# An attention and gMLP block on one core: loads placed behind the end of a unit's turns, and two pairs of neighbouring units by rows in each group

## Chip, cores, metric

The kernel runs on one core of one Trainium2 chip. The metric is the device time of one execution in microseconds (us), as the median of several executions.

## The reference, cut to what matters

```python
x = A_x                                       # 2048 x 512, bf16
# ... (sa, ca, ga, sb, cb, gb) = six vectors of 512 from silu(c) @ w_mod
h = _layernorm(x) * (1 + ca) + sa
q = (h @ wq)                                  # 32 heads of 128; 8 groups of 4 heads share one K, V
scores = einsum('bhqd,bhkd->bhqk', q, k) * Dh ** (-0.5)      # 2048 keys
o = einsum('bhqk,bhkd->bhqd', softmax(scores), v)
x = x + ga * (o @ wo)                         # o: 2048 x 4096
# ... then layernorm and a gMLP: gelu, layernorm over half the channels,
#     a 2048 x 2048 product over positions, a gate, an output product
```

The attention is some 85% of the time, and the change is in it alone.

## The kernel before: the parts that matter

The attention is cut into 128 **units**: 8 groups (one K, V head each) of 16 units, a unit being 128 queries for the four heads of a group. One pass of the main loop, an **iteration**, has eight slots. In a slot TensorE computes an eighth of the scores of the newest unit, an eighth of a V product of an earlier unit, and one matmul of the query or output projection. ScalarE takes the exponential of the slot's scores. Groups and the units of a group are numbered from 0; groups 1 to 6 are the steady middle.

There are two kinds of units. A unit **by columns** gets its scores transposed (keys on partitions), so that its V product can follow at once; but this product needs 64 matmuls of 129 columns. A unit **by rows** gets scores with queries on partitions; each head's rows are normalised on VectorE and then transposed by DMA (a **turn**, four of them per unit). After that its V product needs only 16 matmuls of 512 columns.

```python
TURN_A, TURN_B = 2 * CT, NU - 2                 # 8 and 126
def by_rows(u):
    return TURN_A <= u < TURN_B and u % 2 == 0
def pv_at(u):                                   # iteration of the V product
    return u + 3 if by_rows(u) else u + 1
def wo_at(u):                                   # iteration of the output projection
    return pv_at(u) + (3 if u < TURN_B - CT else 2)
# ...
# in qk(u, i), by rows: two score matmuls, one exponential with its row sum
    nc.scalar.activation(out=rows_of(u, hh)[...], in_=s_ps[:], func=ACT.Exp,
        scale=inv_sqrt_dh, accum_out=rsums[u][:, i : i + 1])
    if half == 1:                               # a head is complete: its turn, two slots later
        at(*divmod(u * NSLOT + i + 2, NSLOT), lambda: turn_rows(u, hh))
# ...
def turn_rows(u, hh):
    # ... tot, reciprocal, rows * rinv on VectorE
    nc.sync.dma_start_transpose(out=pTs[u][:, :, hh * P : (hh + 1) * P], in_=rows)
# ...
# in pv(u, i), by columns, at the last slot: the unit's output is turned as well
    nc.sync.dma_start_transpose(out=oTs[u][:], in_=onorms[u][:].rearrange("p r d -> p (r d)"))
# ...
for g in range(1, HKV):                         # loads of the next groups, on GpSimd's and SyncE's queues
    it = (g - 1) * NT
    at(it + 9, 5, lambda g=g: load_k(g))
    at(*((5, 2) if g == 1 else (it + 7, 4)), lambda g=g: load_wq(g, nc.gpsimd))
    at(*((5, 2) if g == 1 else (it + 11, 4)), lambda g=g: load_v(g))
    at(*((5, 2) if g == 1 else (it + 13, 4)), lambda g=g: load_wo(g, nc.gpsimd))
```

`at(it, slot, fn)` puts a piece of program at a slot. The score banks `s_ps` are two. In the profile lines, the buffers `pT` and `wsp` hold what a V product reads, and `pn`, `win_sb` and `wmod_a` rows that are not turned yet; `x2` marks two instructions merged into one line.

## Time and profile before

| | |
|---|---|
| time | 1314.3 us median of 4 (1313.1 to 1316.1) |
| TensorE busy | 99% |
| ScalarE, VectorE busy | 85%, 53% |
| groups 1 to 6 (iterations 16 to 111) | 837.1 us, 139.52 each |
| DMA engines, mean share in groups 2 to 6 | 0.79 |

The length of a group is the sum of its iterations, and an iteration runs from its first score weight load to the next one's. The view of stretches for groups 2 to 6 of the kernel before: its columns are the stretch and its length, then busy us (and instructions) of TensorE, its weight loads, VectorE, ScalarE and GpSimd, then the granted TensorE clock, the DMA share and GB/s.

```profile
288.38:985.98 697.60, 692.55 (x5026) 395.47 (x5121) 339.47 (x840) 680.60 (x961) 13.65 (x19) 1.00 0.79 143
```

697.60 us for five groups is 139.52 each.

### The profile page before, as it was taken

How to read it: one execution, taken by the hardware profiler on the slowest of the kernel's cores; microseconds unless marked ns; L12 is line 12 of the kernel's file. 1: busy time of each engine (PE TensorE's matmuls, PEld its weight loads, DVE VectorE, ACT ScalarE, POOL GpSimd, SP SyncE). 2: the span in 40 equal slices, each digit the busy share in tenths (PEclk: the TensorE clock that was granted, in tenths of full speed). 3: DMA queues.
4: the chain of work that ended last, by engine and by line, in shares of the span. 5: the costliest groups of instructions: out<-in, count | busy, mean ns of one | idle time of the engine just before them, and what ended most of it. 6: DMA issues, size and time to landing. Idle time of an engine off the chain costs nothing.

```text
span 1312.3 us, 24168 instructions
## 1 busy us (share of the span) xinstructions
PE 1294.0 (99%) x9355; PEld 736.5 (56%) x9527; DVE 689.3 (53%) x1693; ACT 1113.0 (85%) x1533; POOL 55.7 (4%) x96
## 2 busy tenths in 40 slices
PE   9999999999999999999999999999999999999998
PEld 5665555555555555555555555555555555644445
DVE  5644545444445554444545444444454588784444
ACT  7899999999999999999999999999999999550000
POOL 1200000000000000000000000000000011120000
PEclk9999999999999999999999999999999999999999
DMA  6599778878787787879886788678866688365300
GB/s 181 122 117 179 127 142 144 156 122 149 153 161 140 139 142 141 142 138 140 157 162 121 143 142 156 125 146 153 153 130 127 117 143 149 96 134 96 82 21 27
DMA packets 607723, 174.45 MB, mean 133 GB/s; under 512 B 597264, under 2 KB 603664, under 8 KB 607600
## 3 DMA queue, kind: packets, MB, share of 16 engines
q1 hardware_dynamic: 600576, 153.67, 66.1%
q0 software_dynamic: 4432, 16.91, 4.9%
q10 hardware_dynamic: 2592, 2.23, 0.5%
q8 instruction: 77, 1.26, 0.4%
q14 instruction: 46, 0.38, 0.1%
HBM read 21.89 MB, written 2.10 MB: 18 GB/s over the span
## 4 chain that ended last, share of the span: by engine, by line
PE 96%; DMA 1%; issue 1%; DVE 1%; ACT 0%; SPq 0%; POOL 0%; DVEq 0%; ACTq 0%
PE o_ps L1080 19%; PE s_ps L1024 18%; PE s_ps L1005 16%; PE o_ps L1059 15%; PE misc L1112 8%; PE misc L945 8%; PE misc L1437 7%; PE s_ps L1271 2%; PE s_ps L1310 2%; PE o_ps L1458 1%; DMA wsp<-in_w_mod_dram 1%; PE s_ps L1458 0%; DMA kT<-in_A_k_cache_dram 0%; DVE hT L814 0%; DMA hT<-xn 0%
## 5 line engine op out<-in xcount | busy, mean ns | idle before, releaser
L1031 ACT ACTIVATE pT<-s_ps 128x1024 bf16<-128x1024 f32 x552 | 561.1, 1025 | 31.5 <-PE s_ps L1024 9.5
L1080 PEld LDWEIGHTS <-pT 128*128 128x128 bf16 x4416 | 295.3, 98 | 128.9
L1080 PE MATMUL o_ps<-v,pT 128*128 128x129 bf16 x4416 | 339.7, 220 | 1.5
L1024 PE MATMUL s_ps<-qT,kT 128*128 128x512 bf16 x1104 | 328.1, 379 | 1.4 <-ACT pT L1031 0.2
L1005 PE MATMUL s_ps<-kT,qT 128*128 128x512 bf16 x917 | 274.9, 379 | 3.0
L1012 ACT ACTIVATE win_sb<-s_ps 128x1024 bf16<-128x1024 f32 x238 | 243.7, 1025 | 3.5
L1112 PE MATMUL misc<-wo_g,oT 128*128 128x512 bf16 x468 | 177.4, 379 | 0.6
L945 PE MATMUL misc<-hT,wq_g 128*128 128x512 bf16 (+2 forms) x482 | 173.3, 370 | 0.8
L1024 PEld LDWEIGHTS <-kT 128*128 128x128 bf16 x1104 | 107.2, 98 | 115.0 <-issue 2.3
L1012 ACT ACTIVATE pn<-s_ps 128x1024 bf16<-128x1024 f32 x156 | 159.6, 1025 | 2.0 <-ACT wmod_a L1012 0.3
L1059 PEld LDWEIGHTS <-v 128*128 128x128 bf16 x944 | 92.3, 98 | 111.5
L956 DVE CAST qT<-misc 128x512 bf16<-128x512 f32 x125 | 85.7, 685 | 122.9 <-PE misc L945 122.8
L1068 DVE CAST oT<-o_ps 128x512 bf16<-128x512 f32 x59 | 40.8, 692 | 194.9 <-PE o_ps L1059 157.4
L1059 PE MATMUL o_ps<-wsp,v 128*128 128x512 bf16 x457 | 137.1, 379 | 0.6
L1059 PE MATMUL o_ps<-pT,v 128*128 128x512 bf16 x441 | 133.0, 379 | 0.6
L1005 PEld LDWEIGHTS <-qT 128*128 128x128 bf16 x944 | 92.2, 98 | 61.6
L1045 DVE TENSOR_TENSOR tot<-rs 128x1 f32<-128x1 f32 x236 | 36.2, 153 | 127.2 <-ACT win_sb L1012 84.8
L1437 PE MATMUL misc<-wsp,z 128*128 128x512 bf16 (+2 forms) x554 | 101.1, 336 | 0.6 <-issue 0.2
L1050 DVE TENSOR_SCALAR win_sb<-win_sb,rall 128x2048 bf16<-128x2048 bf16 x119 | 89.6, 753 | 4.4 <-DVE rall L1048 0.3
L1012 ACT ACTIVATE wmod_a<-s_ps 128x1024 bf16<-128x1024 f32 x78 | 79.9, 1024 | 0.0
L1437 PEld LDWEIGHTS <-z 128*128 128x128 bf16 x560 | 50.5, 98 | 49.3 <-DVE z L686 1.4
L1125 DVE TENSOR_TENSOR xacc<-misc,xacc 128x512 f32<-128x512 f32 x112 | 76.1, 680 | 0.0
(107 smaller groups left out, 817.3 us busy)
## 6 DMA issues: line engine op xcount, KB each, us to landing
wq_g<-in_A_wq_dram POOLq DMA_DIRECT2D x7, 512.0 KB, 6.2
v<-in_A_v_cache_dram POOLq DMA_DIRECT2D x7, 512.0 KB, 6.9
wo_g<-in_A_wo_dram POOLq DMA_DIRECT2D x7, 512.0 KB, 8.4
wsp<-in_w_mod_dram POOLq DMA_DIRECT2D x1, 2048.0 KB, 11.2
out_dram<-yout ACTq DMA_DIRECT2D x16, 128.0 KB, 1.7
win_sb<-in_B_w_in_dram POOLq DMA_DIRECT2D x1, 1792.0 KB, 8.0
x_sb<-in_A_x_dram SPq DMA_DIRECT2D x3, 512.0 KB, 5.9
oT<-onorm SPq DMA_TRANSPOSE x69, 2.8
```

What stands on the lines that cost most here:

```text
L945: nc.tensor.matmul(ps[0][:, o0 : o0 + n], lhsT=wqs[g][:, dt, hh * DH : (hh + 1) * DH], rhs=hTs[ch][:, dt, c0 : c0 + n], start=(dt == 0), s ...
L956: nc.vector.tensor_copy(out=dst, in_=src)
L1005: nc.tensor.matmul(s_ps[:, c * 512 : (c + 1) * 512], lhsT=qTs[b][:, hh, jj * P : (jj + 1) * P], rhs=groups[g]["kT"][:, k0 : k0 + 512], sta ...
L1012: nc.scalar.activation(out=rows_of(u, hh)[:, half * HK : (half + 1) * HK], in_=s_ps[:], func=ACT.Exp, scale=inv_sqrt_dh, accum_out=rsums[u ...
L1024: nc.tensor.matmul(s_ps[:, h * 512 : (h + 1) * 512].rearrange("p (r q) -> p r q", r=REP), lhsT=groups[g]["kT"][:, kt * P : (kt + 1) * P], ...
L1031: nc.scalar.activation(out=pTs[u][:, 2 * i : 2 * i + 2, :], in_=s_ps[:].rearrange("p (k q) -> p k q", k=2), func=ACT.Exp, scale=inv_sqrt_dh,)
L1050: nc.vector.tensor_scalar(out=rows, in0=rows, scalar1=rinv, scalar2=None, op0=ALU.mult)
L1059: nc.tensor.matmul(o_pss[u][:], lhsT=groups[g]["v1"][:, kt, 0:DH], rhs=pTs[u][:, kt, :], start=(kt == 0), stop=(kt == NKT - 1),)
L1080: nc.tensor.matmul(o_ps[:, hh % 2, 0 : DH + 1], lhsT=pTs[u][:, kt, hh * P : (hh + 1) * P], rhs=groups[g]["v1"][:, kt, 0 : DH + 1], start=( ...
L1112: nc.tensor.matmul(X_ps[:], lhsT=oTs[u][:, hh, :], rhs=groups[g]["wo"][:, hh, :], start=(hh == 0), stop=(hh == REP - 1),)
L1125: nc.vector.tensor_tensor(out=xaccs[j][:], in0=X_ps[:], in1=xaccs[j][:], op=ALU.add)
L1437: nc.tensor.matmul(g_ps[:, :n], lhsT=z2[:, st, f * P : (f + 1) * P], rhs=wsp[t][:, st, c0 : c0 + n], start=(st == 0), stop=(st == NT - 1 a ...
```

## The change

Its intent: more units by rows (59 become 65, by making units 4, 5 and 13, 14 of groups 1 to 6 neighbours by rows), which saves TensorE time (an iteration with a V product by rows took 8.63 us, one by columns 8.81); some V products after two iterations, to keep one per iteration; the load of K two iterations later; and the loads of V, wq and wo held back until the last turn of a certain unit has landed, by a copy on GpSimd that reads what that turn writes.

```diff
-    def by_rows(u):
-        return TURN_A <= u < TURN_B and u % 2 == 0
-    def pv_at(u):
-        return u + 3 if by_rows(u) else u + 1
+    kinds, pv_its = [False] * NU, {}
+    for u in range(TURN_A, TURN_B):
+        pair = NT <= u < NU - NT and u % NT in (5, 6, 13, 14) and not kinds[u - 2]
+        kinds[u] = not kinds[u - 1] or pair
+    by_rows, order = kinds.__getitem__, [(u + 3 if kinds[u] else u + 1, u) for u in range(NU)]
+    order.sort()
+    for it in range(1, NU + 2):
+        due = [u for t, u in order if t <= it]
+        if not due and it > TURN_A + 1:
+            due = [u for t, u in order if t <= it + 1 and kinds[u]]
+        for u in due[: 2 if it > TURN_B else 1]:
+            pv_its[u] = it
+            order = [o for o in order if o[1] != u]
+    pv_at = pv_its.__getitem__
 ...
+    def after_rows(u):
+        seen = stat.tile([1, 1], BF16, name="seen")
+        nc.gpsimd.tensor_copy(out=seen[:], in_=pTs[u][0:1, NKT - 1, 511:512])
+    def after_pv(u):
+        seen = stat.tile([1, 1], FP32, name="seen")
+        nc.gpsimd.tensor_copy(out=seen[:], in_=rall[0:1, u * REP : u * REP + 1])
+    at(5, 0, lambda: after_pv(3))
     for g in range(1, HKV):
         it = (g - 1) * NT
-        at(it + 9, 5, lambda g=g: load_k(g))
-        at(*((5, 2) if g == 1 else (it + 7, 4)), lambda g=g: load_wq(g, nc.gpsimd))
-        at(*((5, 2) if g == 1 else (it + 11, 4)), lambda g=g: load_v(g))
-        at(*((5, 2) if g == 1 else (it + 13, 4)), lambda g=g: load_wo(g, nc.gpsimd))
+        at(it + 11, 5, lambda g=g: load_k(g))
+        loads = (load_v(g), load_wq(g, nc.gpsimd), load_wo(g, nc.gpsimd))   # (as lambdas)
+        for k, load in enumerate(loads):
+            if g == 1:
+                at(5, 0, load)
+                continue
+            u = next(u for u in range(it + 4 + 2 * k, NU) if by_rows(u))
+            at(u + 1, 5, lambda u=u: after_rows(u))
+            at(u + 1, 5, load)
```

(The bookkeeping of row buffers and of which units are looked at in an iteration is left out.)

More of the change, by code (lines that the diff above doesn't have):

```diff
@@ L966 @@
     TURN_A, TURN_B = 2 * CT, NU - 2
-    def by_rows(u):
-        return TURN_A <= u < TURN_B and u % 2 == 0
-    def pv_at(u):
-        return u + 3 if by_rows(u) else u + 1
+    kinds, pv_its = [False] * NU, {}
[11 more added lines that the diff above has]
+            order = [o for o in order if o[1] != u]
+    assert len(pv_its) == NU
+    pv_at = pv_its.__getitem__
     def wo_at(u):
@@ L979 @@
     for u in range(NU):
-        homes[u] = min(users, key=lambda k: users[k])
+        homes[u] = min(users, key=users.get)
         assert users[homes[u]] < u
@@ L1038, in rows_of @@
     def rows_of(u, hh):
-        return pn[((u - TURN_A) // 2 * REP + hh) % len(pn)][:, 0:SK]
+        return pn[(sum(kinds[:u]) * REP + hh) % len(pn)][:, 0:SK]
     def turn_rows(u, hh):
@@ L1254 @@
         at(NU + 1 + st // 4, 2 * (st % 4), lambda st=st: load_wsp(wsp[0], 0, st))
+    def after_rows(u):
[5 more added lines that the diff above has]
+    at(5, 0, lambda: after_pv(3))
     for g in range(1, HKV):
         it = (g - 1) * NT
-        at(it + 9, 5, lambda g=g: load_k(g))
-        at(*((5, 2) if g == 1 else (it + 7, 4)), lambda g=g: load_wq(g, nc.gpsimd))
-        at(*((5, 2) if g == 1 else (it + 11, 4)), lambda g=g: load_v(g))
-        at(*((5, 2) if g == 1 else (it + 13, 4)), lambda g=g: load_wo(g, nc.gpsimd))
+        at(it + 11, 5, lambda g=g: load_k(g))
+        loads = (
+            lambda g=g: load_v(g),
+            lambda g=g: load_wq(g, nc.gpsimd),
+            lambda g=g: load_wo(g, nc.gpsimd),
+        )
+        for k, load in enumerate(loads):
[5 more added lines that the diff above has]
+            at(u + 1, 5, load)
     zs = {}
@@ L1361 @@
             zs["z2"] = z2p.tile([P, NT, FH], BF16, name="z2")
-        pvs = [u for u in (it - 5, it - 3, it - 1) if 0 <= u < NU and pv_at(u) == it]
-        wos = [u for u in range(max(it - 6, 0), min(it - 2, NU)) if wo_at(u) == it]
+        pvs = [u for u in range(max(it - 4, 0), min(it, NU)) if pv_at(u) == it]
+        wos = [u for u in range(max(it - 8, 0), min(it - 2, NU)) if wo_at(u) == it]
         wf = [fn for u in wos for fn in wo_proj(u)]
```

## The prediction

> **What bounds the kernel now.** I read the page first, then the timeline of the middle, then the waits and the landings of DMAs.
>
> The page of the kernel before, engine shares (part 1) and the chain that ended last (part 4):
>
> ```profile
> PE 1294.0 (99%) x9355; PEld 736.5 (56%) x9527; DVE 689.3 (53%) x1693; ACT 1113.0 (85%) x1533; POOL 55.7 (4%) x96
> ...
> PE 96%; DMA 1%; issue 1%; DVE 1%; ACT 0%; SPq 0%; POOL 0%; DVEq 0%; ACTq 0%
> ```
>
> TensorE is 99% busy and 96% of the chain, but a modelled end can hide gaps, so I look at starts. In the timeline of TensorE and ScalarE in the fifth of eight groups (start us, length us, what), one unit by rows (L1005, 602.51 to 611.32) is followed by one by columns (L1024, 611.32 to 619.95):
>
> ```profile
> 602.51 0.59 PE L1005 MATMUL s_ps<-kT,qT 128*128 128x512 bf16 x2
> 602.94 0.62 PE L1080 MATMUL o_ps<-v,pT 128*128 128x129 bf16 x8
> 603.40 0.38 PE L945 MATMUL misc<-hT,wq_g 128*128 128x512 bf16 x1
> 603.61 0.59 PE L1005 MATMUL s_ps<-kT,qT 128*128 128x512 bf16 x2
> ...
> 611.32 0.59 PE L1024 MATMUL s_ps<-qT,kT 128*128 128x512 bf16 x2
> 611.75 0.59 PE L1059 MATMUL o_ps<-pT,v 128*128 128x512 bf16 x2
> 612.18 0.38 PE L945 MATMUL misc<-hT,wq_g 128*128 128x512 bf16 x1
> 612.40 0.59 PE L1024 MATMUL s_ps<-qT,kT 128*128 128x512 bf16 x2
> ...
> 619.95 0.59 PE L1005 MATMUL s_ps<-kT,qT 128*128 128x512 bf16 x2
> ```
>
> Each turn of the loop ("iteration", eight slots) computes one unit's scores (L1005 by rows, L1024 by columns) and the product with V of an earlier unit. The V product of a unit by columns is eight 129-column matmuls a slot (603.40 - 602.94 = 0.46 us, 57 ns each). That of a unit by rows is two of 512 columns (612.18 - 611.75 = 0.43 us). So a slot lasts 1.10 or 1.08 us and an iteration 8.81 or 8.63 us, with every start butting on the one before. I worked out all 128 iterations this way, from the weight loads of L1005 and L1024, of which none is missing: in groups 1 to 6 (numbered from 0) they are 8.81 and 8.63 without one exception, 139.52 us a group. **In these groups TensorE waits for nothing.** That includes the moments when loads collide with turns (a turn is the transpose of one head's rows by DMA):
>
> ```profile
> 611.79 0.76 POOL L739 DMA_DIRECT2D wo_g<-in_A_wo_dram  x1 [24.66 <-PE misc L1112]
> ```
> ```profile
> 616.12 7.26 SPq L1051 DMA_TRANSPOSE wsp<-wmod_a  x1
> 624.05 4.90 SPq L1051 DMA_TRANSPOSE pT<-pn  x2
> ```
>
> The load of wo starts as soon as the old buffer is free, the fourth turn of unit 68 is then issued for 7.26 us (1.3 to 3.5 is usual) and lands 24.6 us after that unit's scores began. Its V product comes three iterations after, at 26.1 us, so nothing is lost. Of the landings of a fourth turn I list: unit 4 of a group (wo collides) 18.5 to 24.6 us, unit 10 (wq collides) 17.6 to 22.2; units 6, 12 and 14, with no load near, 18 cases, median 17.5, mean 17.7, longest 18.3.
>
> [...] one 512 KB load from the POOL queue put off a turn by up to 7 us. [...] Here 57 and 216 are what a sustained stream shows[...].
>
> **The change part by part.**
> (1) *More units by rows.* Running the schedule's few lines by hand gives 59 units by rows before and 65 after: one more in each of the six groups 1 to 6. Neighbours by rows are units 4, 5 and 13, 14 of each. Each extra one replaces 64 matmuls of 129 columns by 16 of 512 (the built program has 576 fewer rows on TensorE: 6 x 48 matmuls with their weight loads, twice). On the path it is worth 8.81 - 8.63 = 0.18 us: **6 x 0.18 = -1.1 us**. It adds four multiplies of 0.75 us on VectorE (53% busy) and four turns of some 2.4 us of DMA, both beside the matmuls; the DMA engines' mean share in the groups goes from about 0.80 to an estimate of 0.86.
> (2) *Two iterations per group (12 in all) have scores by rows and a V product by rows.* There ScalarE may be the slower:
>
> ```profile
> 603.14 1.02 ACT L1012 ACTIVATE win_sb<-s_ps 128x1024 bf16<-128x1024 f32 x1
> 604.06 0.20 ACT L1012 ACTIVATION_READ_ACCUMULATOR win_sb<-s_ps 128x1 f32 x1
> 604.24 1.02 ACT L1012 ACTIVATE win_sb<-s_ps 128x1024 bf16<-128x1024 f32 x1
> ```
>
> An exponential with its row sum takes 1.10 us from start to start, eight take 8.84, TensorE needs 8.63: 0.2 us short. There are two score banks; by the records the score matmuls come 0.25 us after the exponential that frees their bank has ended, so most of the 0.2 is taken up by that reserve and given back in the next iteration by columns (exponentials 1.03 us apart). I put 0.03 us on each: 12 x 0.03 = **+0.4 us**; 2.4 would be the most.
> (3) *Twelve units (4 and 13 of each group) have their V product two iterations after their scores, not three.* It starts 8.81 + 8.63 + 0.43 (the two score matmuls of the slot) = 17.87 us after the scores. Of the 18 undisturbed landings a third came later than that, by 0.08 us averaged over all 18. 12 x 0.08 = **+0.9 us**. This takes for granted that no load falls there.
> (4) *The loads.* V, wq and wo of the next group wait for the last turn of units 4, 7 and 9 to land, K moves from iteration 9 to 11. TensorE waits for no load now, so this saves nothing by itself; it keeps loads out of (3). V falls on unit 5's turns, but that has three iterations: about 18.3 us plus up to 7 is 25.3, against 26.1 and more. The new loads of group 1 start when unit 3's V product is done and are needed at iteration 12: hidden.
> Sum: -1.1 + 0.4 + 0.9 = +0.2 us, so 1315.0 us.
>
> **The rivals.**
> *A: the two-iteration units wait in earnest.* For: 17.5 against 17.87 is a reserve of 0.4 us, and unit 13 follows K, wo and unit 11's turns closely; one collision as before costs 4.5 to 7 us. Against: K is issued well before, and I find unit 11 landed by about 21 us, 3.5 us into unit 13, whose first turn is ready at 4.3. If half of the six units 13 lose 3 us, +9 us: 1324.
> *B: ScalarE becomes the bound in the pairs* and doesn't find the reserve: +2.4 instead of 0.4, 1317.
> *C: the gain is clean:* the landings come by 17.5 as most late ones did: 1313.7.
> *D: loads come too late for the next group.* Against: wq lands about iteration 10 and is needed at 12; V and wo later still. I give it 2%.
>
> **Range and chances.** Three runs of before spread 3 us (1313.1 to 1316.1), so C, my sum and B can't be told apart by one median. Low 1312.6 (C with a good run), high 1319.5 (B, or A in a small part). 2% is 26 us: the gain can't reach it, as the part that changes on the path is 1 us; a loss needs 12 waits of over 2 us each.
>
> **What would show it.** After: iterations of 8.81 and 8.63 again, with the twelve by-rows-by-rows ones at 8.63 to 8.84 (step 2); the group at about 139.3 us + waits; gaps on TensorE before L1059's counterpart in iterations 6 and 15 of a group (step 3), of 0 to 0.4 us; loads starting just past the turns of units 4, 7 and 9 (step 4). I would be wrong if TensorE showed gaps of over 1 us there, if the landings of units 4 and 13 moved past 18.5 us, or if units 5 or 14 were late too.

## More of the kernel before

All DMA transposes, turns and outputs alike, go through SyncE's queue in program order.

## The result

The changed kernel took **1316.24 us** (1315.3 to 1316.6, 4 runs) against 1314.3; the ratio is 1.0012, with a 95% interval of 0.9995 to 1.003. A ratio here is the mean time of one kernel's runs over that of the other's of the same rounds, so not quite the ratio of the medians. The interval takes in 1: the whole times alone don't tell the two kernels apart, and what follows rests on their profiles. The time lies in the predicted range, 1.2 us above the predicted value.

The page of the changed kernel, shares and chain:

```profile
PE 1303.7 (99%) x9239; PEld 723.9 (55%) x9239; DVE 713.0 (54%) x1747; ACT 1113.2 (85%) x1581; POOL 59.0 (4%) x115
...
PE 95%; DMA 3%; DVE 1%; issue 0%; ACT 0%; POOL 0%; SPq 0%; DVEq 0%; ACTq 0%
```

TensorE's share of the chain fell by one point, and DMA's rose from 1% to 3%. The stretch of groups 2 to 6, as shown for before:

```profile
289.48:988.54 699.06, 697.71 (x4881) 384.81 (x4880) 359.27 (x885) 681.12 (x1001) 17.13 (x35) 1.00 0.88 158
```

Five groups now take 699.06 us instead of 697.60, though five extra units by rows should have made them 0.9 us shorter. The DMA share went from 0.79 to 0.88.

The profiled execution is 1.9 us longer (1314.2 against 1312.3): 0.4 us before iteration 16, 2.2 us in groups 1 to 6 (839.3 against 837.1) and -0.6 us in the end part (rounded each). The first and last vary by as much among the profiles here without a change to those parts (147.9 to 149.5 us, and 325.6 to 326.3 us). So the account is that of groups 1 to 6, by iterations:

| groups 1 to 6 | before | after |
|---|---|---|
| by-rows scores, by-columns V product | 48 x 8.81 | 42 x 8.81 |
| by-columns scores, by-rows V product | 48 x 8.63 | 42 x 8.63, 9 of them longer |
| by-rows scores, by-rows V product | none | 12 x 8.63 |
| sum without waits | 837.1 | 836.0 |
| waits of TensorE | 0 | 3.2 |

All the waits are at the V product of units 4 and 13 of a group, those with two iterations instead of three. Over 0.2 us were five: 1.06, 0.57, 0.51, 0.31 and 0.26. The largest, in group 6, in the chain of the changed kernel (start us, length us, what):

```profile
975.54 4.88 DMA wsp<-pn
980.42 0.14 issue
980.56 0.59 PE o_ps L1071 x2
```

The fourth turn of unit 109 is issued at 975.54, lands 4.88 us later, and the V product starts right then. Without a wait its first matmul would have come at 979.50, two score matmuls (0.43 us) behind the last start before it, at 979.07. So the wait is 1.06 us. The waits view gives less:

```profile
PE o_ps L1071 <- DMA wsp<-pn: 0.9, 1, 0.9
...
PE o_ps L1071 <- DMA pT<-pn: 0.8, 2, 0.4
```

Those are 1.7 us of 3.2. A 512-column matmul is drawn 0.38 us long and the next starts after 0.216, so a wait must be over 0.16 us to leave any gap. **Count starts, not gaps, when waits are small.**

Here is a neighbouring pair: iteration 69, with scores by rows (L1017) and the V product by rows (L1071), in TensorE's timeline; 612.86 is the first slot whose V product is the cheaper one.

```profile
612.86 0.59 PE L1017 MATMUL s_ps<-kT,qT 128*128 128x512 bf16 x2
613.29 0.59 PE L1071 MATMUL o_ps<-pT,v 128*128 128x512 bf16 x2
...
613.94 0.59 PE L1017 MATMUL s_ps<-kT,qT 128*128 128x512 bf16 x2
...
615.02 0.59 PE L1017 MATMUL s_ps<-kT,qT 128*128 128x512 bf16 x2
...
621.49 0.59 PE L1036 MATMUL s_ps<-qT,kT 128*128 128x512 bf16 x2
```

From 612.86 to 621.49 is 8.63 us: slots of 1.08. And ScalarE in the same iteration:

```profile
613.49 1.02 ACT L1024 ACTIVATE pn<-s_ps 128x1024 bf16<-128x1024 f32 x1
614.41 0.19 ACT L1024 ACTIVATION_READ_ACCUMULATOR pn<-s_ps 128x1 f32 x1
614.57 1.02 ACT L1024 ACTIVATE pn<-s_ps 128x1024 bf16<-128x1024 f32 x1
...
615.65 1.02 ACT L1024 ACTIVATE pn<-s_ps 128x1024 bf16<-128x1024 f32 x1
```

The exponentials now come 1.08 us apart, not 1.10. So the 1.10 that the prediction took for ScalarE's own speed was TensorE's pace, and ScalarE kept up. The shortest steps between two such exponentials in the records are 1.00 us, so even 1.08 isn't its limit.

The loads start where they were meant to. GpSimd in group 3:

```profile
481.73 0.18 POOL L1270 COPY seen<-wsp 1x1 bf16<-1x1 bf16 x1 [94.13 <-DMA wsp<-wmod_a]
...
482.29 1.16 POOL L729 DMA_DIRECT2D v<-in_A_v_cache_dram  x1 [0.25 <-issue]
```

### The profile page after: what moved, and what is told of

Same layout as the page of the kernel before. It is cut to its first block, busy times and chain, and to the rows that moved or that the text cites. A ratio compares the mean times of both kernels' runs of the same rounds, so it can differ in the third digit from the quotient of the medians.

```text
span 1314.2 us, 23930 instructions
## 1 busy us (share of the span) xinstructions
PE 1303.7 (99%) x9239; PEld 723.9 (55%) x9239; DVE 713.0 (54%) x1747; ACT 1113.2 (85%) x1581; POOL 59.0 (4%) x115
## 4 chain that ended last, share of the span: by engine, by line
PE 95%; DMA 3%; DVE 1%; issue 0%; ACT 0%; POOL 0%; SPq 0%; DVEq 0%; ACTq 0%
PE s_ps L1017 17%; PE o_ps L1092 17%; PE o_ps L1071 17%; PE s_ps L1036 16%; PE misc L1124 8%; PE misc L945 8%; PE misc L1468 7%; PE s_ps L1302 2%; PE s_ps L1341 2%; PE o_ps L1489 1%; DMA wsp<-in_w_mod_dram 1%; DMA pT<-pn 1%; DMA wmod_a<-in_w_mod_dram 1%; PE s_ps L1489 1%; DMA wsp<-pn 0%; DMA wsp<-wmod_a 0%
## 5 line engine op out<-in xcount | busy, mean ns | idle before, releaser
L1043 ACT ACTIVATE pT<-s_ps 128x1024 bf16<-128x1024 f32 x432 | 438.0, 1025 | 28.6 <-PE s_ps L1036 11.2
L1017 PE MATMUL s_ps<-kT,qT 128*128 128x512 bf16 x1040 | 309.3, 379 | 0.0
L1036 PE MATMUL s_ps<-qT,kT 128*128 128x512 bf16 x1008 | 299.6, 379 | 0.3 <-ACT pT L1043 0.2
L1092 PEld LDWEIGHTS <-pT 128*128 128x128 bf16 x3456 | 231.0, 98 | 100.6
L1024 ACT ACTIVATE win_sb<-s_ps 128x1024 bf16<-128x1024 f32 x262 | 267.9, 1024 | 3.6 <-ACT pn L1024 0.3
L1092 PE MATMUL o_ps<-v,pT 128*128 128x129 bf16 x3456 | 265.7, 220 | 0.0
L1124 PE MATMUL misc<-wo_g,oT 128*128 128x512 bf16 x512 | 194.0, 379 | 0.0
L1071 PE MATMUL o_ps<-pT,v 128*128 128x512 bf16 x608 | 180.8, 379 | 0.8 <-DMA pT<-pn 0.8
L1024 ACT ACTIVATE pn<-s_ps 128x1024 bf16<-128x1024 f32 x172 | 175.8, 1023 | 1.9 <-ACT pn L1024 0.3
L1071 PEld LDWEIGHTS <-v 128*128 128x128 bf16 x1040 | 101.2, 98 | 126.4 <-issue 5.8
L1017 PEld LDWEIGHTS <-qT 128*128 128x128 bf16 x1040 | 101.6, 98 | 76.5
L1071 PE MATMUL o_ps<-wsp,v 128*128 128x512 bf16 x432 | 127.8, 379 | 1.1 <-DMA wsp<-pn 0.9
L1043 ACT ACTIVATE wsp<-s_ps 128x1024 bf16<-128x1024 f32 x72 | 73.6, 1023 | 4.1 <-PE s_ps L1036 1.1
```

Of the source, the lines that this page charges most:

```text
L1017: nc.tensor.matmul(s_ps[:, c * 512 : (c + 1) * 512], lhsT=qTs[b][:, hh, jj * P : (jj + 1) * P], rhs=groups[g]["kT"][:, k0 : k0 + 512], sta ...
L1024: nc.scalar.activation(out=rows_of(u, hh)[:, half * HK : (half + 1) * HK], in_=s_ps[:], func=ACT.Exp, scale=inv_sqrt_dh, accum_out=rsums[u ...
L1036: nc.tensor.matmul(s_ps[:, h * 512 : (h + 1) * 512].rearrange("p (r q) -> p r q", r=REP), lhsT=groups[g]["kT"][:, kt * P : (kt + 1) * P], ...
L1043: nc.scalar.activation(out=pTs[u][:, 2 * i : 2 * i + 2, :], in_=s_ps[:].rearrange("p (k q) -> p k q", k=2), func=ACT.Exp, scale=inv_sqrt_dh,)
L1071: nc.tensor.matmul(o_pss[u][:], lhsT=groups[g]["v1"][:, kt, 0:DH], rhs=pTs[u][:, kt, :], start=(kt == 0), stop=(kt == NKT - 1),)
L1092: nc.tensor.matmul(o_ps[:, hh % 2, 0 : DH + 1], lhsT=pTs[u][:, kt, hh * P : (hh + 1) * P], rhs=groups[g]["v1"][:, kt, 0 : DH + 1], start=( ...
```

## The experiments

Why did the twelve units wait 3.2 us and not 0.9? SyncE's queue around unit 109 of the changed kernel shows a candidate (start us, time in issue us):

```profile
970.18 3.94 SPq L1063 DMA_TRANSPOSE wsp<-pn  x1
974.22 1.22 SPq L1112 DMA_TRANSPOSE oT<-onorm  x1
975.54 1.79 SPq L1063 DMA_TRANSPOSE wsp<-pn  x1
```

The fourth turn (975.54) stands behind the transpose of another unit's output (oT), which nobody needs for three iterations. **Theory Q**: this order makes the fourth turn late. **Rival D**: the DMA engines are too full in the pairs, and data would land late in any order. Both lead to the same result; an edit of the order tells them apart.

In each run below, "groups" means the length of groups 1 to 6 in its profile: 837.1 before, 839.3 after, 836.0 if nothing waits with 65 units by rows.

### The changed kernel once more

No edit.

> The changed kernel once more, on the same chip as the next three. Groups 1 to 6 took 839.3 us in its first profile against 837.1 before and 836.0 if no unit waited. Both theories: again 838 to 841 us, all of the excess in the iterations where units 4 and 13 of a group have their V product, 1314.5 to 1317 us in all.

Measured: 1315.90 us, ratio to before 1.0014 (0.9999 to 1.0028); groups 839.1. The long waits stand at the same units with nearly the same lengths (group 6 unit 13: 1.19 us, 1.06 the first time; units 13 of groups 1 and 3: 0.55 and 0.53, 0.57 and 0.51 the first time). They are part of the schedule and not chance. Those of units 4 are less firm: 0.7 us together the first time, 0.2 us now.

### oT behind the fourth turn

```diff
-            oTs[u] = late.tile([P, REP, P], BF16, name="oT", bufs=5)
-            nc.sync.dma_start_transpose(out=oTs[u][:], in_=onorms[u][:]...)
+            def turn_out():
+                oTs[u] = late.tile([P, REP, P], BF16, name="oT", bufs=5)
+                nc.sync.dma_start_transpose(out=oTs[u][:], in_=onorms[u][:]...)
+            if TURN_A < pv_at(u) < TURN_B:
+                at(pv_at(u) + 1, 2, turn_out)
+            else:
+                turn_out()
```

> The changed kernel with the transpose of a unit's output (oT, needed three iterations later) issued behind the fourth turn of the next unit by rows instead of ahead of it. Theory Q (the fourth turn lands late because it stands behind oT in SyncE's queue, where oT's issue takes 1.2 to 2.0 us): the fourth turn is issued at 11.2 to 12.5 us instead of 13.2 to 14.2, lands at 15.6 to 17.3, all before 17.87; no iteration is over 8.81 or 8.63, groups 1 to 6 take 836.0 us, total some 1313. Rival D (the DMA engines are fuller in the pairs, so that data lands late whatever the order): the fourth turn is issued earlier but still lands at 17.5 to 19, groups 1 to 6 stay at 838 to 840.

Measured: 1313.45 us, ratio 0.9995 (0.998 to 1.0011); groups **836.1**, every iteration 8.81 or 8.63. A second run on another chip:

> The changed kernel with oT behind the fourth turn, once more, to narrow its time: groups 1 to 6 at 836.1 us as in its first run, 1.0 us below the kernel before; total 0.5 to 1.5 us below it. If the gain were only in its first run's profile: no wait-free groups this time, 838 us.

Measured: **1312.02 us** (1311.5 to 1312.6) against 1313.61 of before on that chip, ratio 0.9988 (0.9975 to 1.0); groups 836.1 again. SyncE at the same place of the first run, unit 109:

```profile
968.29 6.18 SPq L1063 DMA_TRANSPOSE wsp<-pn  x2
974.52 1.44 SPq L1113 DMA_TRANSPOSE oT<-onorm  x1
```

The third and fourth turns are one row now, with oT behind. In the twelve units the fourth turn was issued 11.4 to 13.2 us after the scores began, against 13.2 to 14.2. The last landings that the two runs' records show were 16.3 to 17.8 us; V products start at 17.87. Q holds for these waits: D wanted the landings unmoved. The proof is in the groups, two profiles of each kernel (839.3 and 839.1, then twice 836.1). In the whole time the intervals of the two kernels overlap.

### One more transpose ahead of the fourth turn

```diff
+            if NT <= pv_at(u) < NU - NT and pv_its.get(pv_at(u)) == pv_at(u) + 2 and kinds[pv_at(u)]:
+                spare = late.tile([P, REP, P], BF16, name="oTspare", bufs=1)
+                nc.sync.dma_start_transpose(out=spare[:], in_=onorms[u][:]...)
```

> The changed kernel with one idle transpose of the same output more, into a spare tile, ahead of the fourth turn of units 4 and 13 alone (12 in all). Theory Q: each of the twelve fourth turns is issued and lands 1.3 to 2 us later, TensorE waits 1.3 to 2 us longer at each, groups 1 to 6 take 839.3 + 12 x 1.3 to 2.0 = 855 to 863 us, total 1331 to 1340. Rival D: 128 KB more for the DMA engines is some 0.6 us each, 12 x 0.6 = 7 us at most, total 1319 to 1323.

Measured: 1329.34 us, ratio 1.0114 (1.0095 to 1.0132); groups 852.9, 16.9 us over the wait-free 836.0 or 1.4 us per unit, against 0.27 in the changed kernel.

```profile
982.40 3.21 SPq L1063 DMA_TRANSPOSE wsp<-pn  x1
985.71 1.42 SPq L1112 DMA_TRANSPOSE oT<-onorm  x1
987.18 1.26 SPq L1117 DMA_TRANSPOSE oTspare<-onorm  x1
988.54 2.75 SPq L1063 DMA_TRANSPOSE wsp<-pn  x1
```

The spare one takes 1.36 us of the queue from start to start, and a unit lost 1.1 us more on average. That is a little below the 1.3 that Q named, and twice what D allowed (7 us in all, 13.7 measured); the groups lie outside both expected ranges, nearer to Q's (855 to 863 us) than to D's. So most of the time added to the queue ahead of the fourth turn went into the wait. Unit by unit it was anything from 0.1 us (group 6 unit 13, the longest wait before) to 2.0, so the queue's time isn't simply added.

### Two iterations, but no neighbours

```diff
+    kinds = [TURN_A <= u < TURN_B and u % 2 == 0 for u in range(NU)]
+    by_rows = kinds.__getitem__
+    pv_its = {u: u + 3 if kinds[u] else u + 1 for u in range(NU)}
+    for u in range(NT, NU - NT):
+        if u % NT in (4, 12):
+            pv_its[u], pv_its[u + 1] = u + 2, u + 3
```

(in place of the changed kernel's schedule; its loads are kept)

> 59 units by rows, none beside another, new loads; but units 4 and 12 of each group have their V product two iterations after their scores and the units by columns behind them also two after. Asks whether the short distance alone costs what the changed kernel lost, or whether the second unit by rows beside it is needed. Theory Q (the queue order oT, then the fourth turn, with 0.4 us to spare): waits of 0 to 0.5 us at some of the twelve, 1 us in all by the landings of units 6, 12 and 14 before (groups 1 to 6 at 838 us), total 1314 to 1316. Rival D (the second unit's turns fill the DMA engines and are the cause): no wait at all, 837.1 us.

Measured: 1314.85 us, ratio 1.0011 (0.9997 to 1.0026); groups 837.9, so 0.8 us of waits, in three of the twelve units above all (0.46, 0.16 and 0.14). This is close to what the landings of the kernel before gave (1 us). So the short distance costs 0.8 us here, and 3.2 in the changed kernel, with the same order of oT and the fourth turn: the order alone doesn't make the 3.2. It is tempting to put the rest down to the neighbours, but the run moved half of the units too (12 in place of 13). Units 4 are alike in both: 0.5 us here, 0.7 and 0.2 in the two profiles of the changed kernel, so in them no cost of a neighbour shows. The rise is in units 13 (2.5 us) against units 12 (0.3), and whether the neighbour or the place does it stays open. The prediction's method was sound, but its sample, units 6, 12 and 14 of a schedule without neighbours, was not that of the new schedule.

### Only the new places of the loads

The schedule of before (the first three added lines above), the loads of after.

> Only the new places of the loads; units by rows and their V products as before (59 by rows, all three iterations later). Prediction's step 4 (the loads are hidden in either place): groups 1 to 6 take 837.1 us as before, iterations of 8.81 and 8.63 without exception, time within 1 us of before. Rival (the loads now come late for their group, or collide where they matter): iterations over 8.81 near iteration 12 or at the start of a group, 1 us or more lost.

Measured: 1314.59 us, ratio 1.0003 (0.9989 to 1.0016); groups 837.1 without one long iteration. The places of the loads alone are worth nothing either way, as step 4 said.

### The pairs with the loads in their old places

The loads' lines of before put back into the changed kernel.

> The new units by rows and V products, with the loads where they stood before. Prediction's step 4 (the new places keep loads out of the way of the units with two iterations): wo starts at the beginning of iteration 5 of each group again and pushes unit 4's fourth turn to 18.5 to 24.6 us, as it did in the kernel before, so TensorE waits 1 to 7 us at iteration 6 of each group, 23 us over the six by the landings of before; units 13 wait 2.8 us together as now; groups 1 to 6 take some 861 us, total 1336 to 1341. Rival (the loads do no harm in the old places either, they only jitter): 838 to 841 us, 1315 to 1317.

Measured: **1354.60 us**, ratio 1.0311 (1.0296 to 1.0326); groups 878.5. The fourth turn of unit 4 landed at 19.9 to 25.5 us in the six groups. By the starts of their V products these six units waited 29.5 us, more than the 23 expected, and the six iterations were 39.7 us over their 8.63. Where the other 10.2 us went shows in the stretches of group 2: the iteration before the wait, the wait, and two stretches after it.

```profile
336.02:344.65 8.63, 8.63 (x44) 3.92 (x42) 6.01 (x16) 8.62 (x17) 0.76 (x1) 1.00 1.15 133
344.65:352.68 8.03, 0.81 (x5) 0.23 (x4) 2.27 (x5) 1.87 (x3) 0.00 (x0) 0.88 1.37 142
352.68:358.04 5.36, 5.36 (x14) 1.96 (x15) 0.00 (x0) 1.93 (x2) 0.00 (x0) 0.54 1.13 212
358.04:363.06 5.02, 5.02 (x25) 2.26 (x24) 0.69 (x1) 4.46 (x6) 0.00 (x0) 1.00 0.86 158
```

For 5.4 us after the wait the granted clock (third column from the right) is 0.54, and the same matmuls take twice as long (in the chain two score matmuls take 0.85 us there and 0.43 us from 358.04 on). Over this run, the one on the old loads below, the one with two of three and the one with an extra transpose, the clock was about 0.5 after all six waits of 4.6 to 7.7 us and after three of five between 2.5 and 2.8 us, but after none of up to 2.1 us (mean granted clock of the four profiled runs, in this order: 0.988, 0.992, 0.998 and 0.999). A halved clock cost 1.7 to 2.4 us on top of the wait. I hadn't reckoned with it in any estimate.

SyncE in that iteration shows what wo's load, issued at 336.69, does to a turn (its issue takes 9.28 us, 1.8 is usual):

```profile
341.23 9.28 SPq L1063 DMA_TRANSPOSE pT<-wmod_a  x1
```

### oT behind the fourth turn, with the loads in their old places

> oT behind the fourth turn, loads where they stood before. Asks whether the 2 us won in the queue make the new places of the loads needless. If wo's load delays the fourth turn of unit 4 by 1 to 7 us as before, 2 us cover some of it: waits of 0 to 5 us in units 4, some 12 us over six groups, none in units 13: groups at 845 to 852 us, total 1322 to 1330. Rival (the earlier issue lets the fourth turn slip in ahead of the load): no wait, 836.0 us, 1313.

Measured: 1337.92 us, ratio 1.02 (1.0174 to 1.0226); groups 859.5, and units 13 without a wait. It is worse than I expected: two of the six units 4 waited over 5 us, and the halved clock came on top (mean granted clock 0.992 in the profiled run, against 0.999 with the loads in their new places). The gain of 2 us in the queue doesn't make the new places of the loads needless. The places cost nothing and guard the short distances.

### Two of every three units by rows

Since units with two iterations cost nothing in the right order, how far can it be taken? With oT behind:

```diff
-        pair = NT <= u < NU - NT and u % NT in (5, 6, 13, 14) and not kinds[u - 2]
-        kinds[u] = not kinds[u - 1] or pair
+        kinds[u] = not (kinds[u - 1] and (kinds[u - 2] or not NT <= u < NU - NT))
```

> oT behind the fourth turn, and two of every three units by rows in groups 1 to 6 (75 in all, 32 of them with two iterations). If TensorE stays the bound: groups 1 to 6 take 836.0 - 10 x 0.174 = 834.3 us, total some 1311.5, with iterations of 8.63 wherever scores and V product are both by rows, which also asks again whether ScalarE keeps up. If the DMA engines become the bound (mean share 0.80 with 48 units by rows in these groups, 0.88 with 54, so some 1.0 with 64): turns queue up, the fourth turns land later from unit to unit, and groups take 145 us and more, total over 1340.

Measured: 1327.68 us (1322.9 to 1331.5), ratio 1.0097 (1.0075 to 1.0119); groups 853.9. It is neither: the DMA share was 1.01, as the second theory had it, yet groups took 142.3 us each, between the two theories' 139.05 and 145, and 84 of 96 iterations had no wait. Those that waited for a V product belong to units 6, 8, 10, 11 and 12 of a group, where V, wq, wo and K are loaded, but for one of 0.6 us at a unit 2. One more, of 1.25 us in group 1, is another kind: the scores of unit 7 waited for ScalarE, which by the waits view waited 1.6 us for a buffer of rows whose turn, issued just after V's load, had not landed. So I asked whether it is the loads again:

```diff
-        pair = NT <= u < NU - NT and u % NT in (5, 6, 13, 14) and not kinds[u - 2]
+        pair = NT <= u < NU - NT and (u + 3) % NT < 10 and not kinds[u - 2]
```

(in the kernel with oT behind)

> oT behind the fourth turn, and two of every three units by rows only from unit 12 of a group to unit 6 of the next (71 in all, the ones with two iterations at units 2, 5, 12 and 15); from 7 to 11, where V, wq, wo and K are loaded, by turns as before. Theory (in the run with two of three throughout, the waits come from loads falling on units with two iterations, not from the DMA engines being full): no wait, groups 1 to 6 take 836.0 - 6 x 0.174 = 835.0 us, total some 1312.5. Rival (the DMA engines are full): waits at units 2, 5, 12 and 15 too, groups 838 us and more.

Measured: 1321.56 us, ratio 1.0066 (1.0053 to 1.0079); groups **835.2** with no wait over 0.04 us, at a DMA share of 0.97. About the groups the theory was right. The time is a miss: the part from unit 112 on took 335.3 us instead of 325.6 to 326.3. The odd number of pairs had shifted the alternation, so that unit 125 was by rows, and its rows live in the buffer that B_w_in is loaded into. That load started at 1118.4 us, 134.2 us after iteration 112 began (1111.9 and 125.9 in the kernel before), and the waits view of this run has 4.4 of the 9 us that were lost:

```profile
PE s_ps L1308 <- DMA win_sb<-in_B_w_in_dram: 4.4, 1, 4.4
```

One pair fewer (`NU - NT - CT` as the upper limit, 70 by rows) puts the last unit by rows back to 124:

> As the run before with two of three from unit 12 to unit 6, less one pair of neighbours (70 by rows), so that the last unit by rows is 124 again and not 125. In that run groups 1 to 6 took 835.2 us without a wait, but the part after unit 112 took 335.0 us against 325.6 to 326.3 in all others: unit 125 by rows holds the buffer that B_w_in is loaded into, so that load started 6 us later and TensorE waited. Theory (only the end was lost): groups 835.3 us, end 325.7 us, total 1311 to 1312, the fastest of all. Rival (more units by rows cost something at the end or elsewhere as well): end over 328 us, total over 1314.

Measured: 1313.24 us, ratio 0.9992 (0.9978 to 1.0005); groups 835.4, end 326.9 us. The 8 us are back, so it was the end's schedule. The end was 1.2 us longer than I expected, which I leave open, and the total missed the expected 1311 to 1312. It can't be told from the kernel with oT behind (0.9995 and 0.9988 in its two runs). Both have shorter groups than the kernel before, by 1.0 and 1.8 us in every profile; in the time, 0.1% is at the edge of what 5 rounds resolve.

## Why the prediction was right, step by step

**The bound** (TensorE, waiting for nothing): right. Every run without waits has iterations of 8.81 and 8.63 to 0.01 us.

**Step 1** (six more units by rows, -1.1 us): right. Where the waits are removed, the groups are 1.0 us shorter than before.

**Step 2** (ScalarE behind in twelve iterations, +0.4 us): wrong, mechanism and size. It measured 0: all twelve took 8.63. The error was to read a duration from a spacing: exponentials 1.10 us apart next to slots of 1.10 us say nothing of how fast ScalarE could go. The rival built on the same number, that ScalarE becomes the bound, falls with it; the reserve wasn't needed.

**Step 3** (twelve V products after two iterations, +0.9 us): mechanism right, size wrong. It measured 3.2 us, 0.27 per unit instead of 0.08, and 2.5 of it in units 13. The sample of landings had a mean of 17.7 us; in the new schedule the fourth turns of units 13 landed at 18.4 us on average and those of units 4 at 18.0. "I would be wrong if" named 18.5 us: three of the twelve passed it (18.6, 18.6 and 19.0), and they cost 2.1 of the 3.2. Its other sign, a gap of over 1 us on TensorE, came once: 1.06 us by the starts, drawn as 0.90. Only the order of oT and the fourth turn was shown to cause the wait, by taking it away and by doubling it; the run without neighbours shows that it takes something besides the order. Why units 13 are later than units 4 stays open: in the changed kernel's profile their third turns were 2.8 to 4.0 us in issue, against 1.5 to 3.4, and no run was made on that.

**Step 4** (the loads are hidden either way and guard step 3): right. The new places alone changed nothing, and without them the pairs cost 40 us. "A loss needs 12 waits of over 2 us each" was wrong in its sum: six waits did it. They were 4.9 us long on average (29.5 together), and the drop of TensorE's clock after five of them added 10.2.

Sum: -1.1 + 0 + 3.2 = +2.1 by the terms as measured, and +2.2 measured in the groups; predicted +0.2. The two wrong terms had opposite signs (0.4 too much, 2.3 too little) and were small, so the range held. But the range, drawn for the spread of the runs and for the rivals, takes in the unchanged kernel's 1314.3 as well: that the time fell into it says little for the steps, which only the iterations and the experiments tested.

Small slips in the working changed nothing: eight steps of 1.10 us are 8.80, not 8.84; the score matmuls of a slot start 0.44 to 0.55 us after the exponential that frees their bank (medians by slot in the kernel before; 0.17 at the least), not 0.25; and the V product of unit 68 starts 26.7 us after its scores (602.51 to 629.19), not 26.1. My estimates of 2.4 us of DMA for a turn in step 1, and of 0.6 us for 128 KB in the run with an extra transpose, were low: in groups 2 to 6 of the kernel before, the queue with the turns moved 91.79 MB in 74.1% of the 16 engines' 697.6 us, which is 2.9 us for 512 KB and 0.7 us for 128 KB.

**The rivals.** A (a collision at units 13 in earnest) had the place right and the size wrong: units 13 lost 2.5 us together, not 9, and only one of them over 1 us. C (the gain is clean) was not what the change did, but is what it does with oT behind. D (loads too late for the next group) showed nowhere; the only load that came late was another, in an experiment's end part.

## What to carry to other kernels

When one engine is the bound and waits for nothing, a change that only thins the reserves of others brings at most its direct saving and puts all of that at risk: compare the landing of what is waited for with the moment it is needed, and ask what stands ahead of it in its queue. An item of a queue that is needed late should not stand ahead of one that is needed at once; here that move took away 3.2 us of waits, where the change saves 1.1 us of work. A spacing between instructions need not be the instruction's own speed: the exponentials came 1.10 us apart beside slots of 1.10, 1.08 beside slots of 1.08, and 1.00 at the shortest.

## What the traces showed of the hardware

- TensorE's pace: streams with a weight load per matmul kept 57 ns from start to start at 129 columns and 216 ns at 512 through whole groups (medians in groups 1 to 6 of both kernels).
- The granted clock: 0.54 for 5.4 us after a stretch of 8.03 us in which TensorE was busy for 0.81 (the pairs on the old loads). The price was 1.7 to 2.4 us on top of the wait where the clock was halved, which came after six of six waits of 4.6 to 7.7 us, three of five of 2.5 to 2.8 us and none of up to 2.1 us.
- Issuing DMA transposes: a 512 KB turn mostly held SyncE's queue for 1.3 to 4.0 us (median 1.9 to 2.0 in the groups of the two kernels), and 9.28 us beside a 512 KB load from another queue in the run with the pairs on the old loads; a 128 KB one (oT) held it for 1.2 to 2.0 us mostly. This, and the order in the queue, decided the case.
- The accumulator read that follows an exponential with a row sum took 0.19 us and began 0.1 us before the exponential's end. Steps of 1.08 us for 1024 columns were kept for whole iterations, and single ones of 1.00 us occurred.
